# Plan's deadlines shifted by groups, scores of two batches turned by transposes, plan's durations set anew

## The chip, the cores and the metric

The kernel runs on one core of a Trainium2 chip. The metric is the device time of one execution in microseconds (us). The engines are named as in the profile: PE is TensorE (PEld its weight loads), ACT is ScalarE, DVE is VectorE, POOL is GpSimd, SP is SyncE, which issues all DMAs here. PSUM is the memory that PE writes its sums to, SBUF the one that the engines read their operands from.

## The reference

```python
B, H, S, Ns, D = (8, 8, 512, 32, 64)                     # x: B,H,S,D   state: B,H,Ns,D
...
scores = scale * np.matmul(x, state.transpose(0, 1, 3, 2))
a = softmax(scores)          # over Ns, max taken out, 1e-9 in the sum
xread = np.matmul(a, state)
scores2 = scale * np.matmul(state, x.transpose(0, 1, 3, 2))
a2 = softmax(scores2)        # over S
sread = np.matmul(a2, x)
attn = np.concatenate([xread, sread], axis=2)
...
x = attn.transpose(0, 2, 1, 3).reshape(B * 544, 512)     # tokens
a = x @ w_a                                              # 512 x 1536
b = x @ w_b
return (a * b) @ w_out                                   # 1536 x 512
```

`scores2` is `scores` with its two last axes exchanged. The softmaxes run along different axes of the same numbers.

## The kernel before, in words

**Numbers.** Everything is float32. The large matmuls run in a one-pass format (fp32r) that holds the high part of a number; each operand is split into a high and a low part (`p_h`/`p_l`, `at_h`/`at_l`, `g_h`/`g_l`, the two halves of `wq`, `wo`), and a product is made of three matmuls (high x high, high x low, low x high). Small matmuls, as the scores, run on plain float32.

**Two products joined.** `xread` is not made. For a batch, the state times the weights (`project`, tiles `ms` or `acc` in PSUM, then `sw_st`, `wo10`, `wo11` in SBUF) goes to DRAM (`scr`), comes back as a piece `p_raw` (`Batch.load`), and is split into `p_h` and `p_l` (`Batch.split`). Layer 1 multiplies the attention weights `at_h`, `at_l` with these pieces (`layer1`, PSUM tiles `ab`), makes `g = a * b` on ACT and DVE, and layer 2 (`layer2`, PSUM tiles `acc`) multiplies `g` with `w_out`. `VISITS` says in which order batches and chunks of the hidden width (0 to 5) are met; the 256 state rows of all batches (`States`) come last. Batch 0's chunk 0 and batch 2's chunk 1 don't go through DRAM (`direct0`, `direct1`).

**Attention** (`class Attention`, two groups `g` of four heads for each of eight batches; `attend`). For batches 0 and 1 (`WIDE`) the scores are made twice: `scores` gives them with the 32 states on partitions and 512 tokens along the row (PSUM tile `ms`, two matmuls 64x512), `scores_t` gives the same numbers with tokens on partitions (eight matmuls 128x64). From the second, `soft_t`, `exp`, `norm` and `back_t` make `at_h` and `at_l`, with PE turning them back by transposes against `ident`. From the first, `soft` makes `e2`, `reads` turns it by four transposes into `a2`, `sread` multiplies it with `x_nat` and `keep` puts the result into `xst`. The other six batches make the scores once, and DVE turns them in blocks of 32.

**What sets the order.** The program is recorded first, one `Unit` per instruction or per group that must stay together, with an engine, a duration `occ` and a latency `lat` from `cost`. `plan` builds the dependences, gives each unit a latest start `late` (backwards from the layer matmuls, whose due times `base` are paced), and then runs forward: on each engine it takes, among the units that can start, the one with the smallest `late`. The instructions are emitted in the order found. On the chip each engine runs its instructions in this order, so what stands ahead of a waiting instruction decides who else waits. Queues that matter here: PE, ACT, DVE, and SP for the DMAs. The pool `ps_ms` has two PSUM banks: a third group of products can start only when ACT has copied the first.

Every instruction is emitted by one line (1049), so the profile's groups are told apart by tile names. `wo` in the profile stands for `wo0` to `wo11`, and for the buffers `wo6`, `wo8` to `wo11` that other data use early.

Of the kernel before, what the change touches and what calls it, by code (L numbers as in the profile page):

```python
# [18 lines left out]
B, H, S, NS, D = 8, 8, 512, 32, 64  # L19
DM, DFF = 512, 1536  # L20
P = 128
# [143 lines left out]
class Recorder:  # L165
# [29 lines left out]
    def cost(self, u, eng, method, out, ins, kw):  # L195
        n = 1
        sh = (out if isinstance(out, View) else ins[0]).where()[0]
        for x in sh[1:]:
            n *= x
        ps = bool(ins) and ins[0].tile.pool.name.startswith("ps")  # L200
        if eng == "PE":
            if method == "transpose" or kw.get("is_transpose"):
                o = n * .85
            elif ins[-1].dtype == F32R:
                o = n * .4535
            else:
                o = n * 1.82
            if sh[0] < P:
                o *= sh[0] / P
            lat = o + 172  # L210
        elif eng == "ACT":
            if method == "activation":
                o, lat = (870, 960) if "accum_out" in kw else (560, 660)
            elif ps:
                o, lat = 466 * n / 512 + (60 if n < 300 else 0), 587 * n / 512 + (80 if n < 300 else 0)
            else:
                o, lat = 522 * n / 512, 100 + n * 1.015
            if n < 8:
                o, lat = 60, 80
        elif eng == "DVE":  # L220
            if method.startswith("tensor_scalar") and not ps:
                o, lat = (65, 140) if n <= 1 else (75, 166) if n <= 16 else (333 * n / 512, 419 * n / 512)
            elif method == "tensor_reduce":
                o, lat = 593, 676
            elif method == "transpose":
                o, lat = 628, 704
            elif method == "reciprocal":
                o, lat = (72, 154) if n == 1 else (162, 244)
            else:
                o, lat = 65 + n * 1.045, 155 + n * 1.045  # L230
        elif eng == "SP":
            o = 440
            v = out if isinstance(out, View) else ins[0]
            u.bytes = 4
            for x in v.where()[0]:
                u.bytes *= x
            u.load = isinstance(out, View) and out.tile.pool.name != "dram"
            lat = 1000 + u.bytes / 345 + (1400 if u.load else 750)
        else:
            o, lat = 1000, 1060  # L240
        if eng in ("ACT", "DVE") and out.tile.name.startswith("sd_") and len(out.where()[0]) == 4:
            o, lat = 2 * o, 2 * lat
        if eng in ("ACT", "DVE"):
            o, lat = o * SLACK, lat * SLACK
        if u.calls[:-1]:
            u.lat = u.occ + lat
            u.occ += o
        else:
            u.occ, u.lat = o, lat
# [10 lines left out]
WAKE, SLACK = 500, 1.1  # L260
# [2 lines left out]

def plan(units, pools, t0):

    n = len(units)
# [37 lines left out]
    left = [len(x) for x in suc]  # L306
    order = [i for i in range(n) if not left[i]]
    late = [0.0] * n
    end = max(u.base for u in units if u.base is not None) + 20e3
    k = 0  # L310
    while k < len(order):
        i = order[k]
        k += 1
        u = units[i]
        d = end if u.base is None else u.base + t0
        for j, wait in suc[i].items():
            d = min(d, late[j] - (0 if not wait else u.occ if units[j].eng == u.eng and u.eng != "SP" else u.lat + WAKE))
        late[i] = d
        for j in pre[i]:
            left[j] -= 1  # L320
            if not left[j]:
                order.append(j)
# [3 lines left out]
    wait = [len(x) for x in pre]  # L326
# [4 lines left out]
    done = [None] * n  # L331
    start = [None] * n
    seq, out, lanes, dma = 0, [], [], 0.0
# [5 lines left out]
    def slot(i, t):  # L339

        for x in opens.get(i, ()):
            q = slots.setdefault((x.pool, x.name), [])
            if len(q) < x.bufs:
                continue
            free_at = [max(done[j] for j in h.uses) for h in q if all(done[j] is not None for j in h.uses)]
            if not free_at:
                return None
            t = max(t, min(free_at) + WAKE)
        return t

    while len(out) < n:
        best = None
        for e in engines:
            while known[e] and known[e][0][0] <= free[e]:
                r, i = heapq.heappop(known[e])
# [5 lines left out]
            for l, i in now_ready[e]:  # L361
                t = slot(i, floor)
                if t is not None:
                    cand.append((t, l, i))
            if known[e]:
                lim = min(cand)[0] if cand else None
                for r, i in known[e]:
                    if lim is None or r < lim:
                        t = slot(i, max(r, floor))
                        if t is not None:  # L370
                            cand.append((t, late[i], i))
            if cand:
                t = min(cand)[0]
                c = min((l, i) for x, l, i in cand if x <= t + 1e-6)
# [3 lines left out]
        t, e, i = best  # L378
        u = units[i]
# [19 lines left out]
            q.append(x)  # L399
        out.append(i)  # L400
        for j, w in suc[i].items():
            r = t if not w else t + u.occ if units[j].eng == e and e != "SP" else done[i] + WAKE
            ready[j] = max(ready[j], r)
            wait[j] -= 1
            if not wait[j]:
                heapq.heappush(known[units[j].eng], (ready[j], j))
# [8 lines left out]
def attn_moe(ctx, tc, xt, xn, sd, wl, w_out, out):  # L415
# [32 lines left out]
    ident = const0.tile([P, P], F32, name="ident")  # L448
# [86 lines left out]
    w = {}  # L535
# [48 lines left out]
    def new_a(b):  # L584
        a_t[b] = [att.tile([P, NG, S], F32R, name=n, bufs=3) for n in ("at_h", "at_l")]
# [10 lines left out]
    class Attention:  # L596
# [26 lines left out]

        def scores_t(self, psp, tag):

            self.t = psp.tile([P, 512], F32, name=tag)
            self.sp = att.tile([P, 16, 32], F32, name="s_p")
            with rec.together(self.sp):
                for sb in range(4):
                    for hp in range(2):  # L630
                        c = sb * P + hp * D
                        nc.tensor.matmul(self.t[:, c:c + D], lhsT=self.x[:, hp, sb * P:(sb + 1) * P],
                                         rhs=self.st[:, hp], start=True, stop=True)

        def soft_t(self):

# [103 lines left out]
    class Batch:  # L740
        n, nk = S, NG
# [79 lines left out]
    class States:  # L821
        n, nk, begun = B * NS, 4, False
# [36 lines left out]
    units = [Batch(b) for b in range(B)] + [States()]  # L859
# [77 lines left out]
    def attend(b):  # L937
        if b not in a_t:
            new_a(b)
        for g in range(NG):  # L940
            a = atts[b, g]
            a.load()
            if b in WIDE:
                a.scores_t(*ms)
                a.scores()
                a.soft_t()
                a.exp()
                a.norm()
                a.back_t(*ms)
                a.soft()  # L950
            else:
                a.scores()
                a.soft()
                a.exp()
                a.norm()
                a.back()
            a.nat()
            a.reads()
            a.sread()
            a.keep()  # L960
# [81 lines left out]
    for p in prev:  # L1042
        layer2(*p)
        flush()
    order, start = plan(rec.units, pools, T0)
    with tc.manual_schedule():
        for i in order:
# [44 lines left out]
```

## Time and profile before

| | |
|---|---|
| median of 3 runs | 728.1 us (725.89 to 730.09) |
| the profiled execution's own time | 728.81 us |
| its span, first to last instruction | 727.0 us |
| granted TensorE clock, mean | 0.990 |
| matmul records, DVE, ACT instructions | 3440, 947, 723 |
| DMA | 134.32 MB, 185 GB/s over the span |

A row of the timeline has the start, the time from start to end of the instructions merged in it, the engine, the operation with its tiles (out<-in) and shapes, and how many. In brackets stands the idle time of the engine just before and what ended it. A matmul of 512 columns overlaps its neighbours, so its length is more than its distance to the next. A float32 matmul has two records. A clock of 0.91 in a window of 20 us means that PE ran at half clock for a part of it.

### The profile page before, as it was taken

To read this page: it belongs to the slowest core of one execution; us is meant where nothing else is said; L and a number is where in the kernel's file an instruction comes from. 1 tells how busy PE (TensorE), PEld (TensorE's weight loads), DVE (VectorE), ACT (ScalarE), POOL (GpSimd) and SP (SyncE) were. 2 spreads that over 40 slices of the span, in tenths; PEclk is the share of its full clock that TensorE was granted. 3 is DMA by queue.
4 is the path that set the end of the run, shared out by engine and by line. 5 is a ranking of instruction groups with operands and counts; after the bars stand their busy time and mean duration, and the time that the engine had idled before them with its cause. 6 is when DMAs were issued, how large, how long until landed. Compare 5 with 4: busy or idle time off the path is not lost.

```text
span 727.0 us, 9629 instructions
## 1 busy us (share of the span) xinstructions
PE 699.6 (96%) x3440; PEld 559.9 (77%) x3440; DVE 495.3 (68%) x947; ACT 395.1 (54%) x723; POOL 0.7 (0%) x6
## 2 busy tenths in 40 slices
PE   5798899999899999999999999999999999999997
PEld 4475657787786888888888887887788888988886
DVE  4985886996756967684799547637879833795322
ACT  4965786686955459786445325334456433553222
POOL 0000000000000000000000000000000000000000
PEclk9999999999999999999999999999999999999999
DMA  8557767768979436859988134314416320611002
GB/s 335 206 210 267 249 249 251 262 238 288 318 254 325 161 118 259 282 220 313 380 325 295 53 115 124 116 59 134 165 54 205 120 59 30 200 32 30 1 0 87
DMA packets 55087, 134.32 MB, mean 185 GB/s; under 512 B 5632, under 2 KB 5632, under 8 KB 55040
## 3 DMA queue, kind: packets, MB, share of 16 engines
q1 hardware_dynamic: 55040, 133.71, 52.9%
q8 instruction: 27, 0.44, 0.2%
q14 instruction: 20, 0.16, 0.1%
HBM read 87.03 MB, written 46.66 MB: 184 GB/s over the span
## 4 chain that ended last, share of the span: by engine, by line
PE 91%; ACT 4%; DVE 3%; DMA 1%; issue 1%; SPq 0%; DVEq 0%; ACTq 0%
PE ab L1049 40%; PE acc L1049 38%; PE ms L1049 12%; ACT wq L1049 2%; DMA stg<-xt 1%; DVE t L1049 1%; DVE m L1049 1%; DVE s_p L1049 0%; ACT t L1049 0%; DVE p_l L1049 0%; ACT sd_h L1049 0%; SPq L1049 0%; ACT stg L1049 0%; ACT sw_st L1049 0%; ACT at_h L1049 0%
## 5 line engine op out<-in xcount | busy, mean ns | idle before, releaser
L1049 PE MATMUL acc<-wo,g_h 128*128 128x512 f32 x816 | 255.9, 393 | 0.2 <-DVE wo L1049 0.2
L1049 PEld LDWEIGHTS acc<-wo,g_h 128*128 128x128 f32 x816 | 151.5, 188 | 33.7 <-issue 2.3
L1049 DVE TENSOR_TENSOR a_sb<-ab,a_sb 128x512 f32<-128x512 f32 (+1 forms) x108 | 71.3, 660 | 132.0 <-PE ab L1049 124.0
L1049 PE MATMUL acc<-wo,g_l 128*128 128x512 f32 x408 | 157.4, 392 | 0.0
L1049 PE MATMUL ab<-at_h,p_h 128*128 128x512 f32 x384 | 151.6, 398 | 1.1 <-ACT p_h L1049 1.1
L1049 PE MATMUL ab<-at_l,p_h 128*128 128x512 f32 x384 | 151.3, 394 | 0.0
L1049 PE MATMUL ab<-at_h,p_l 128*128 128x512 f32 x384 | 150.2, 394 | 0.0
L1049 ACT COPY a_sb<-ab 128x512 f32<-128x512 f32 (+1 forms) x108 | 60.9, 564 | 146.2 <-PE ab L1049 145.2
L1049 ACT CAST g_h<-a_sb 128x512 fp32r<-128x512 f32 (+1 forms) x108 | 64.5, 597 | 52.1 <-DVE a_sb L1049 51.7
L1049 PEld LDWEIGHTS acc<-wo,g_l 128*128 128x128 f32 x408 | 76.5, 188 | 16.4 <-issue 1.0
L1049 PEld LDWEIGHTS ab<-at_h,p_h 128*128 128x128 f32 x384 | 72.8, 190 | 19.8 <-ACT p_h L1049 2.7
L1049 PEld LDWEIGHTS ab<-at_h,p_l 128*128 128x128 f32 x384 | 72.5, 189 | 19.6 <-issue 3.0
L1049 PEld LDWEIGHTS ab<-at_l,p_h 128*128 128x128 f32 x384 | 73.0, 190 | 16.1 <-issue 1.8
L1049 DVE TENSOR_TENSOR g_l<-a_sb,g_h 128x512 fp32r<-128x512 f32 (+1 forms) x108 | 70.8, 656 | 20.9 <-ACT g_h L1049 20.8
L1049 DVE TENSOR_TENSOR p_l<-p_raw,p_h 128x512 fp32r<-128x512 f32 x92 | 60.0, 684 | 12.5 <-ACT p_h L1049 12.5
L1049 ACT CAST p_h<-p_raw 128x512 fp32r<-128x512 f32 x92 | 52.9, 621 | 14.9 <-PE ab L1049 9.2
L1049 DVE TENSOR_SCALAR t<-t 128x512 int32<-128x512 int32 x120 | 49.9, 422 | 9.8 <-ACT t L1049 8.9
L1049 PE MATMUL ms<-wq,sd_h 128*128 128x512 f32 (+2 forms) x112 | 39.6, 425 | 7.1 <-ACT wo L1049 3.8
L1049 ACT CAST wq<-t 64x512 fp32r<-64x512 f32 (+1 forms) x64 | 39.4, 619 | 8.3 <-PE ms L1049 2.8
L1049 DVE SCALAR_TENSOR_TENSOR t<-raw,t 128x512 int32<-128x512 int32 (+1 forms) x60 | 39.7, 686 | 0.3
L1049 PE MATMUL ms<-wq,sd_l 128*128 128x512 f32 (+2 forms) x112 | 38.5, 412 | 0.0
L1049 ACT COPY wo<-ms 128x512 f32<-128x512 f32 x44 | 25.8, 591 | 11.5 <-PE ms L1049 10.9
(93 smaller groups left out, 706.9 us busy)
## 6 DMA issues: line engine op xcount, KB each, us to landing
p_raw<-scr SPq DMA_DIRECT2D x46, 512.0 KB, 4.3
scr<-sw_st SPq DMA_DIRECT2D x48, 256.0 KB, 4.1
scr<-wo SPq DMA_DIRECT2D x48, 256.0 KB, 4.2
raw<-wl SPq DMA_DIRECT2D x22, 512.0 KB, 5.7
part<-stg SPq DMA_DIRECT2D x20, 512.0 KB, 2.9
stg<-part SPq DMA_DIRECT2D x20, 512.0 KB, 6.0
out<-stg SPq DMA_DIRECT2D x34, 256.0 KB, 2.3
x_raw<-xt SPq DMA_DIRECT2D x14, 576.0 KB, 3.7
```

The costliest lines, as they stand in the source:

```text
L1049: getattr(obj, method)(*map(real, args), **{k: real(x) for k, x in kw.items()})
```

## The change

It has three parts. First, `plan`'s model: the durations of two kinds of matmul, and the latency between two dependent instructions of ACT or DVE, which is now counted in full. Second, `late` gets an offset per group of units that stand together in the recording; the offsets come out of a fixed list of 54 seeds. Third, in batches 0 and 1 the scores are made once, copied to SBUF by ACT, and turned by four transposes.

```diff
             elif ins[-1].dtype == F32R:
-                o = n * .4535
+                o = (n + 32) / 2.4
             else:
-                o = n * 1.82
+                o = 90 + n * 1.8
...
+MOVES = (
+    3000001, 3000002, 3000012, 3000024, 3000027, 3000035, 3000036, 3000048, 3000052, 3000054, 3000060, 3000078,
...
+def shifts(units):
+    group, last, n = [], None, -1
+    for u in units:
+        n += u.eng == "SP" or u.eng != last
+        last = u.eng
+        group.append(n)
+    c = [0.0] * (n + 1)
+    for seed in MOVES:
...
+        end = (.12 if draw() < .4 else .3 if draw() < .5 else 1.0) * len(c)
+        begin = int(draw() * .8 * end * .6)
+        share = 10 ** (-.5 - 2.5 * draw())
+        far = 1000 * 10 ** (1.2 * draw())
+        for k in range(len(c)):
+            if k >= end:
+                break
+            u, v = draw(), draw()
+            if k >= begin and u < share:
+                c[k] += (2 * v - 1) * far
+    return [c[k] for k in group]
...
+    shift = shifts(units)
...
-            d = min(d, late[j] - (0 if not wait else u.occ if units[j].eng == u.eng and u.eng != "SP" else u.lat + WAKE))
-        late[i] = d
+            d = min(d, late[j] - (0 if not wait else u.lat + WAKE if units[j].eng != u.eng or u.eng == "SP" else
+                                  u.occ if u.eng == "PE" else u.lat))
+        late[i] = d + shift[i]
...
-            r = t if not w else t + u.occ if units[j].eng == e and e != "SP" else done[i] + WAKE
+            r = t if not w else done[i] + WAKE if units[j].eng != e or e == "SP" else t + u.occ if e == "PE" else done[i]
...
         def scores_t(self, psp, tag):
+            sc = self.e2
+            nc.scalar.copy(out=sc, in_=self.s)
+            self.s = sc
             self.t = psp.tile([P, 512], F32, name=tag)
...
                 for sb in range(4):
-                    for hp in range(2):
-                        c = sb * P + hp * D
-                        nc.tensor.matmul(self.t[:, c:c + D], lhsT=self.x[:, hp, sb * P:(sb + 1) * P],
-                                         rhs=self.st[:, hp], start=True, stop=True)
+                    nc.tensor.transpose(self.t[:, sb * P:(sb + 1) * P], sc[:, sb * P:(sb + 1) * P], ident)
...
             if b in WIDE:
+                a.scores()
                 a.scores_t(*ms)
-                a.scores()
```

PE's first rows, before. `x_raw` and `stg` are the inputs of batch 0, `acc<-wq,p_raw` is `direct0`, `s_p` the softmax with tokens on partitions, `ab` layer 1:

```order
L1049 MATMUL ms_114<-x_raw_96 128x64 x8
L1049 MATMUL ms_123<-x_raw_96 64x512 x2
L1049 MATMUL ms_148<-stg_104,stg_100 128x64 x8
L1049 MATMUL acc_182<-wq_158,p_raw_110 32x256 x4
L1049 MATMUL ms_201<-ident_87,s_p_132 128x128 x4
L1049 MATMUL acc_212<-wq_176,p_raw_112 32x256 x4
L1049 MATMUL acc_182<-p_h_208,wo7_94 128x256
L1049 MATMUL ms_201<-at_h_223,wo7_94 128x512
L1049 MATMUL ab_233<-at_h_223,p_h_208 128x512
```

PE's first rows, after the change (`e2` holds the copied scores):

```order
L1092 MATMUL ms_114<-x_raw_96 64x512 x2
L1092 MATMUL ms_127<-ident_87,e2_121 128x128 x4
L1092 MATMUL ms_149<-ident_87,e2_121 128x128 x4
L1092 MATMUL ms_159<-stg_98,stg_100 64x512 x2
L1092 MATMUL ms_170<-x_nat_106,a2_157 64x128 x8
L1092 MATMUL ms_188<-ident_87,e2_180 128x128 x4
L1092 MATMUL acc_211<-wq_164,p_raw_108 32x256 x4
L1092 MATMUL ms_223<-ident_87,s_p_142 128x128 x4
L1092 MATMUL ms_223<-at_h_235,wo7_94 128x512
L1092 MATMUL ab_247<-at_h_235,p_h_239 128x512
```

The eight 128x64 matmuls of each group are gone, four transposes of the copied scores stand in their place, and the reads of the first group (transposes of the finished `e2`, then the product with `x_nat`) have moved ahead of the first `direct0`.

The place where the first products go to DRAM and come back. First ACT's rows before (the copies of the products to `sw_st`, `wo10` and `wo11`; `acc_441` is the last product):

```order
L1049 COPY sw_st_414<-acc_398 128x512
L1049 CAST g_h_436<-a_sb_378 128x512
L1049 COPY wo11_446<-acc_417 128x512
L1049 ACTIVATE t1_454<-wo8_261 128x512
L1049 COPY wo11_446<-acc_441 128x512
```

ACT's rows after (`acc_484` is the last product):

```order
L1092 COPY wo10_454<-acc_438 128x512
L1092 COPY a2_479<-ms_449 128x512
L1092 COPY sw_st_482<-acc_456 128x512
L1092 COPY wo11_491<-acc_474 128x512
L1092 COPY a_sb_498<-ab_337 128x512
L1092 COPY sw_st_482<-acc_465 128x512
L1092 COPY wo11_491<-acc_484 128x512
```

Then SP's queue before (`scr0_0` holds the products, `p_raw` a piece, `raw` a tile of weights to be converted, `x_nat` the tokens for an attention read):

```order
L1049 DMA x_nat_503<-xn 128x1024
L1049 DMA p_raw_516<-scr0_0_349 128x2x512
L1049 DMA p_raw_520<-scr0_0_349 128x2x512
L1049 DMA raw_527<-wl 128x2x512
L1049 DMA part0_0_564<-stg_547 128x1024
```

SP's queue after:

```order
L1092 DMA x_nat_533<-xn 128x1024
L1092 DMA raw_549<-wl 128x2x512
L1092 DMA p_raw_568<-scr0_0_444 128x2x512
L1092 DMA p_raw_572<-scr0_0_444 128x2x512
L1092 DMA part0_1_613<-stg_599 128x1024
```

On ACT a copy for the attention (`a2`) and one for layer 1 (`a_sb`) have come between the copies of the products. On SP the load of weights has moved from behind the two pieces to ahead of them.

PE's rows at the second half of chunk 2's products, before (each pair of `ms` rows is one group of products that ACT must copy away; `ab_1843` is layer 1 on a piece from DRAM):

```order
L1049 MATMUL ms_1797<-wq_1471,sd_h0_180 128x512
L1049 MATMUL ms_1797<-wq_1471,sd_l0_264 128x512
L1049 MATMUL ms_1805<-wq_1471,sd_h0_180 128x512
L1049 MATMUL ms_1805<-wq_1471,sd_l0_264 128x512
L1049 MATMUL ms_1827<-wq_1538,sd_h1_217 128x512
L1049 MATMUL ms_1827<-wq_1538,sd_l1_279 128x512
L1049 MATMUL ms_1834<-wq_1538,sd_h1_217 128x512
L1049 MATMUL ms_1834<-wq_1538,sd_l1_279 128x512
L1049 MATMUL ab_1843<-at_h_1353,p_h_1832 128x512
```

The same products after:

```order
L1092 MATMUL ms_1774<-wq_1416,sd_h0_167 128x512
L1092 MATMUL ms_1774<-wq_1416,sd_l0_231 128x512
L1092 MATMUL acc_1622<-wo2_1066,g_h_1727 128x512 x2
L1092 MATMUL acc_1652<-wo2_1066,g_h_1727 128x512 x2
L1092 MATMUL acc_1672<-wo2_1066,g_h_1727 128x512 x2
L1092 MATMUL ms_1795<-wq_1416,sd_h0_167 128x512
L1092 MATMUL ms_1795<-wq_1416,sd_l0_231 128x512
L1092 MATMUL acc_1609<-wo2_1066,g_l_1784 128x512
L1092 MATMUL ms_1802<-wq_1549,sd_h1_209 128x512
L1092 MATMUL ms_1802<-wq_1549,sd_l1_273 128x512
```

Six groups stood in a row; now layer-2 matmuls stand between them.

More of the change, by code (lines that the diff above doesn't have):

```diff
@@ L261, with draw @@
 LOOSE = ("stg",)
+MOVES = (
[5 rows of a table added]
+)
+def shifts(units):
[6 more added lines that the diff above has]
+    for seed in MOVES:
+        x = seed * 2654435761 + 12345 & 0xFFFFFFFF
+        def draw():
+            nonlocal x
+            x = x * 1664525 + 1013904223 & 0xFFFFFFFF
+            return (x >> 8) / 2.0 ** 24
+        for _ in range(4):
+            draw()
+        end = (.12 if draw() < .4 else .3 if draw() < .5 else 1.0) * len(c)
[9 more added lines that the diff above has]
+    return [c[k] for k in group]
 def plan(units, pools, t0):
```

4 rows, old and new, of the table MOVES are left out of this document.

## The prediction

> **What bounds the kernel now.** I read the page's first part, then the busy time by stretch, then TensorE's rows with what ended each wait, then the rows of the other engines at the long waits.
>
> ```profile
> PE 699.6 (96%) x3440; PEld 559.9 (77%) x3440; DVE 495.3 (68%) x947; ACT 395.1 (54%) x723; POOL 0.7 (0%) x6
> L1049 PE MATMUL acc<-wo,g_h 128*128 128x512 f32 x816 | 255.9, 393 | 0.2 <-DVE wo L1049 0.2
> 0.00:25.00 25.00, 14.17 (x61) 9.72 (x61) 15.64 (x33) 14.65 (x23) 0.70 (x6) 1.00 0.80 304
> 25.00:55.75 30.75, 27.57 (x171) 20.46 (x172) 26.62 (x53) 23.11 (x47) 0.00 (x0) 0.94 0.61 212
> 55.75:101.75 46.00, 39.69 (x213) 26.81 (x214) 32.91 (x74) 32.31 (x62) 0.00 (x0) 0.93 0.77 264
> 101.75:187.00 85.25, 82.12 (x381) 63.19 (x382) 68.49 (x133) 59.59 (x109) 0.00 (x0) 0.98 0.75 257
> 187.00:717.00 530.00, 530.00 (x2586) 434.87 (x2585) 349.52 (x654) 264.67 (x485) 0.00 (x0) 1.00 0.47 162
> 717.00:727.00 10.00, 6.06 (x32) 4.87 (x30) 2.14 (x4) 0.78 (x2) 0.00 (x0) 0.97 0.14 52
> ```
>
> The stretches (columns: stretch, length, busy time of PE, PEld, DVE, ACT, POOL, then granted clock and DMA) say where time can be had. From 187 to 717 us PE is busy for 530.00 of 530.00 us at clock 1.00: a new order of the same matmuls can gain nothing there, it can only lose. All idle time of PE lies elsewhere: 10.83 us up to 25, 3.18 to 55.75, 6.31 to 101.75, 3.13 to 187 and 3.94 at the end. Beside it stands lost clock, 0.91 to 0.98 after waits. So the span is the sum of PE's work and of what PE waits for in the first 187 us.
>
> **Part 1: scores made once, then turned.** For batches 0 and 1 the second set of score matmuls goes (eight per attention, 128x64), and four transposes of the copied scores take its place.
>
> ```profile
> 34.38 0.60 PE L1049 MATMUL ms<-ident,e 128*128 128x128 f32 x4
> 34.73 0.36 PE L1049 MATMUL acc<-p_h,wo 128*128 128x256 f32 x1
> 34.93 1.89 PE L1049 MATMUL ms<-x_raw 128*128 128x64 f32 x16
> 36.63 0.48 PE L1049 MATMUL ab<-at_h,p_h 128*128 128x512 f32 x1
> ```
>
> Start to start, eight such matmuls (16 records) hold PE for 36.63 - 34.93 = 1.70 us, and four transposes for 34.73 - 34.38 = 0.35 us. That is 1.35 us of PE per attention, 5.4 us for four; 2.7 of it (batch 1) lies where PE is nearly always busy. Batch 0's share lies in the head, where PE waits anyway. Added are four copies on ScalarE (0.59 us each, 0.48 where they follow each other: two in 1.07 us, a row below). They stand in the chain scores, copy, transposes, softmax, so in the head they lengthen it.
>
> TensorE: Matmul & The Clock Gate in the Trainium skill, section "Part 4: PE-mode transpose", speaks against this part: a 128x128 transpose takes some 275 ns in a kernel, and transposes do not count as work that releases the clock. By its time, an estimate, four cost 1.1 us and batch 1 saves 1.2 instead of 2.7 us. The rows above differ: four take 0.35 us between their neighbours. Its second half returns as a rival.
>
> **Part 2: the order at the head.**
>
> ```profile
> 4.38 5.58 PE L1049 MATMUL ms<-x_raw 128*128 128x64 f32 x20 [4.38 <-DMA x_raw<-xt]
> 10.24 3.65 PE L1049 MATMUL ms<-stg 128*128 128x64 f32 x16 [0.28 <-DMA stg<-xt]
> 19.77 1.09 PE L1049 MATMUL ms<-ident,s_p 128*128 128x128 f32 x4 [4.65 <-DVE s_p L1049]
> 22.61 0.63 PE L1049 MATMUL ab<-at_h,p_h 128*128 128x512 f32 x1
> 25.14 0.66 PE L1049 MATMUL ms<-ident,s_p 128*128 128x128 f32 x4 [1.50 <-ACT at_l L1049]
> ```
>
> PE starts when the first load lands (4.38) and reaches the first layer-1 matmul at 22.61. Followed by hand in the new order with the rows' durations, ScalarE has copy, exp, two state casts of 1.1 us each and more in front of the first `at_h`, so the first layer-1 matmul comes at about 23.0: nothing won there. But PE's waits are filled: both attention reads of batch 0 and the scores of batch 1 now stand ahead of the state products. I put the end of those products at 43.5 us; now the copy behind the last of them starts at 45.53 (next fence).
>
> **Part 3: the first piece from DRAM.** PE can start batch 0's second chunk of work only when the products have gone to DRAM and come back as `p_raw`.
>
> ```profile
> 45.53 0.59 ACT L1049 COPY wo<-acc 128x512 f32<-128x512 f32 x1 [1.10 <-PE acc L1049]
> 49.41 1.58 SPq L1049 DMA_DIRECT2D p_raw<-scr  x2
> 51.24 0.37 SPq L1049 DMA_DIRECT2D raw<-wl  x1
> 55.08 1.14 ACT L1049 CAST p_h<-p_raw 128x512 fp32r<-128x512 f32 x2 [1.00 <-DMA p_raw<-scr]
> 53.76 1.08 PE L1049 MATMUL ms<-x_raw 128*64 128x512 f32 x4
> 55.75 0.50 PE L1049 MATMUL ab<-at_h,p_h 128*128 128x512 f32 x1 [0.91 <-ACT p_h L1049]
> ```
>
> From the last product's copy (45.53) to the first matmul on its piece (55.75) pass 10.2 us. In the new order this chain gets longer twice: the last product's copy stands behind five other copies on ScalarE (5 x 0.48 = 2.4 us), and on SP the load stands behind `raw<-wl` instead of ahead of it. That load waits for VectorE to finish the tile it overwrites, and its 512 KB go first: nothing if VectorE is early, some 2 us at the 212 to 304 GB/s of these stretches; I take 1. The first matmul then comes at 43.5 + 0.2 + 10.2 + 2.4 + 1 = 57.3 us, 1.5 later than now, and PE stands still there for about 4 us, since the work that it has in between is about 9.5. But by then PE has done 3.8 us of work that now comes later: two attention reads (1.0 each, 58.96 below), scores (1.0, row 53.76) and eight transposes (0.7). **Gain to this point: 3.8 - 1.5 = 2.2 us**; ends -0.5 (the load 2.7 us later still) and 4.7 (`raw` costs nothing and the copies come in time).
>
> **Part 4: the waits behind it.**
>
> ```profile
> 58.96 1.09 PE L1049 MATMUL ms<-wo,a 128*64 128x128 f32 x16 [1.41 <-ACT e L1049]
> 60.37 0.78 PE L1049 MATMUL ms<-ident,s_p 128*128 128x128 f32 x4 [0.31 <-DVE xst L1049]
> 61.82 0.79 PE L1049 MATMUL ms<-at_h,wo 128*128 128x512 f32 x1 [0.46 <-ACT at_h L1049]
> 62.41 1.05 PE L1049 MATMUL ab<-at_h,p_h 128*128 128x512 f32 x2
> 67.97 0.39 PE L1049 MATMUL ms<-wq,sd_h 128*128 128x256 f32 x1 [0.18 <-ACT e L1049]
> ```
>
> The four waits make 2.36 us. The attention work that PE waits for here stands ahead of the piece's first use in the new order, so I take 2.0 of it as gone. From 60.4 on the rows are stretched too (two matmuls in 1.05 us at 62.41), some 1.7 us lost; but a wait of 4 us before it would cost the same again, so I count no gain of clock. **2.0 us**, ends 0 and 3.8.
>
> ```profile
> 87.17 0.39 PE L1049 MATMUL ms<-wq,sd_h 128*128 128x256 f32 x1 [2.05 <-ACT sw_st L1049]
> 88.85 0.58 PE L1049 MATMUL ms<-wq,sd_h 128*128 128x256 f32 x1 [0.24 <-ACT e L1049]
> 96.90 1.09 PE L1049 MATMUL ms<-wq,sd_h 128*32 128x512 f32 x8 [1.49 <-ACT wo L1049]
> 101.75 0.50 PE L1049 MATMUL ab<-at_h,p_h 128*128 128x512 f32 x1 [0.18 <-ACT p_h L1049]
> ```
>
> Here PE waits 3.96 us for ScalarE to empty one of the two `ms` banks: six groups of products stand within 3.2 us of PE's work. After the first wait matmuls run at half clock until 91.2 (1.2 us lost). In the new order a group starts 1.2 to 3.3 us of PE's work behind the one before it (its rows counted at 0.22 us for 512 columns: two matmuls take 0.61 us in the row at 722.44 below, one 0.39). I take 4.2 of these 5.2 us; ends 1 and 5.2, since ScalarE stays loaded (32.31 of 46.00 us).
>
> ```profile
> 179.33 0.50 PE L1049 MATMUL ms<-wq,sd_h 128*128 128x512 f32 x1 [0.27 <-ACT sw_st L1049]
> 180.57 0.50 PE L1049 MATMUL ms<-wq,sd_h 128*128 128x512 f32 x1 [0.50 <-ACT sw_st L1049]
> 183.66 0.80 PE L1049 MATMUL ms<-wq,sd_h 128*128 128x512 f32 x1 [2.36 <-ACT wo L1049]
> 184.25 0.63 PE L1049 MATMUL ms<-wq,sd_l 128*128 128x512 f32 x1
> 183.02 1.07 ACT L1049 COPY wo<-ms 128x512 f32<-128x512 f32 x2
> ```
>
> This is the clearest place. Six product groups stand back to back, and ScalarE puts five steps of a weight conversion between their copies, so the fifth group waits until 183.02. The waits make 3.13 us. Behind them single matmuls take 0.63 us where 0.39 is the mean, for 3.4 us: 1.6 us more. The new order, counted likewise, has 0.2 to 2.5 us of matmuls between such groups, and the piece from DRAM that follows them is wanted 18 us of PE's work after its last product, not 5. I take 4.2 of 4.7; ends 1 and 4.7.
>
> TensorE: Matmul & The Clock Gate in the Trainium skill, section "Why this matters for your kernels", asks for no idle gap above some 3 us to keep the clock. The rows at 60.37 and 184.25 differ: waits of 1.41 and 2.36 us were enough to lose it. By the rule those stretches would have kept their clock, and part 4 would have 2.4 us less to win.
>
> **Part 5: the end.**
>
> ```profile
> 722.44 0.61 PE L1049 MATMUL acc<-wo,g_l 128*128 128x512 f32 x2
> 722.87 1.29 DVE L1049 TENSOR_TENSOR stg<-acc,stg 128x512 f32<-128x512 f32 x2 [2.47 <-PE acc L1049]
> ```
>
> Both last sums end together, so VectorE adds them one behind the other (1.29 us). In the new order the first is finished five matmuls earlier: 0.4 us less. The longer second layer that now closes the program gives ScalarE and VectorE 2.9 us of matmuls to make the last `g` in, and they need about 2: no new wait.
>
> **The plan's other edits** (durations, the latency between two instructions of one engine, the shifts) put no instruction in; they act through the order alone. Against all this stands what I couldn't follow row by row: new waits, above all in the 530 us that have none. Between 0 and 6 us; I take 1, as the distance between product groups and from products to pieces there is like before's.
>
> **Sum:** 2.2 + 2.0 + 4.2 + 4.2 + 0.4 - 1.0 = 12.0 us; the 2.7 us of batch 1 are within the first term. The span goes from 727.0 to 715.0. The profiled execution took 728.81, 1.8 over its span, and is 0.7 above the median of 728.1: 715.0 + 1.8 - 0.7 = **716 us**.
>
> **Rivals.**
> - *All waits go, and the load from DRAM is in time:* each term at its good end, 4.7 + 3.8 + 5.2 + 4.7 + 0.4 = 18.8 us, 709. For it: no two product groups on ScalarE's tight places are pressed together any more. Against: the load behind `raw`. 0.18.
> - *The waits only move:* ScalarE is as loaded as before and has four copies more, so PE waits for it at other places. Left are the 2.7 us of batch 1 and little else: 724 to 726. For it: 32.31 of 46.00 us busy on ScalarE in the worst stretch. 0.12.
> - *The head stays at half clock:* transposes take the place of matmuls up to 20 us. The rows up to 22.61 already run at half clock (0.63 for one matmul). If transposes don't keep the clock up, one or two more spells of 3.4 us cost 1.7 each: 718 to 719. The skill's transpose section, above, says so of the clock. 0.08.
> - *Slower:* the first load from DRAM. Each us by which that piece is late is paid in full, since PE's order is fixed and its next row needs it. With 12 us of other gains, and 3.6 more to be seen, it decides from 15.6 us: the piece would have to come at 73 instead of 57, through `raw<-wl` waiting that much longer for VectorE. Then 732. VectorE is busy 26.62 of 30.75 us there, which makes some delay likely and such a one not. 0.04.
>
> The forecast itself has 0.58. **The range** is 707 to 724: the good ends give 709, and head gains that I bounded too tightly a little less; all bad ends together (-0.5 + 0 + 1 + 1 - 6) give 732, and up to 724 leaves about 2 in 10 out on both sides. A measurement of this kernel can tell about 0.5%, 3.6 us, from no change; faster means under 724.5: 0.90 (forecast, first and third rival, half of the second), within 0.06, slower 0.04.
>
> **What would show it.** Right: no wait of PE for ScalarE's copies above 1 us between 70 and 190 us; the stretch from 190 to 715 still full; one wait of 3 to 5 us for `p_h` near 57 us; about 64 records of 128x64 gone. Wrong: a wait of over 2 us in a place that has none now, PE idle after 190 us, or the first layer-1 matmul later than 25 us.

## The result and the profile after

The changed kernel takes 706.1 us, median of four runs (705.07 to 709.38), the kernel before beside it on the same chip 727.2 (725.89 to 730.09): a ratio of 0.9711, interval 0.969 to 0.9732. That is 21 us faster where 12 were forecast, and 0.9 us below the range. The profiled execution took 705.07 us with a span of 703.3; its difference from before's profiled one (span 727.0) is 23.7 us, some 2.6 more than between the medians.

The first part of the page, then the busy time by stretch (columns as before: stretch, length, busy time of PE, PEld, DVE, ACT, POOL, granted clock, DMA):

```profile
PE 686.8 (98%) x3392; PEld 549.6 (78%) x3392; DVE 487.2 (69%) x947; ACT 395.1 (56%) x727; POOL 0.7 (0%) x6
0.00:25.00 25.00, 14.07 (x62) 7.00 (x63) 16.88 (x38) 17.95 (x31) 0.70 (x6) 0.85 0.86 325
25.00:55.75 30.75, 28.73 (x181) 20.18 (x179) 27.73 (x64) 26.93 (x56) 0.00 (x0) 0.96 0.84 290
55.75:101.75 46.00, 46.00 (x265) 33.20 (x264) 42.48 (x91) 38.56 (x72) 0.00 (x0) 1.00 0.84 291
101.75:187.00 85.25, 85.25 (x389) 69.26 (x387) 68.08 (x128) 66.55 (x121) 0.00 (x0) 1.00 0.82 289
187.00:693.00 506.00, 506.00 (x2467) 414.53 (x2467) 329.38 (x622) 243.03 (x446) 0.00 (x0) 1.00 0.46 155
```

From 55.75 us on PE does not wait until the tail, and its clock is full. PE's idle time over the span is 16.5 us instead of 27.4: 10.9 us of the 23.7. Its busy time fell by 12.8. Of this 5.4 are matmul work that is gone (16 records of 128x64 at 0.106 us less four transposes at 0.0875, four times). The other 7.4 us are work that runs in less time. Some 4.4 of them are clock: before had three stretches at half clock behind 55 us, with 2.94, 3.16 and 3.39 us of busy time in them, and 0.46 of that is lost (the last section has the 0.46); the changed kernel has none there.

What is left stands at the head. Some of PE's rows there, with what ended each wait:

```profile
10.24 1.11 PE L1092 MATMUL ms<-ident,e 128*128 128x128 f32 x4 [2.17 <-ACT e L1092]
20.77 0.80 PE L1092 MATMUL ms<-at_h,wo 128*128 128x512 f32 x1 [1.41 <-ACT at_h L1092]
21.67 1.22 PE L1092 MATMUL ab<-at_h,p_h 128*128 128x512 f32 x2
41.86 0.28 PE L1092 MATMUL acc<-wq,sd_l 128*128 128x256 f32 x1
53.86 0.49 PE L1092 MATMUL ab<-at_h,p_h 128*128 128x512 f32 x1 [0.17 <-ACT p_h L1092]
```

The first layer-1 matmul starts at 21.67 (22.61 before), the last product of states and weights at 41.86, and the first matmul on the piece from DRAM at 53.86 (55.75 before), after a wait of 0.17 us. The chain between the last two, from the rows of ACT and SP (`acc` is a product, `a_sb` a copy for layer 1):

```profile
42.18 0.59 ACT L1092 COPY a_sb<-ab 128x512 f32<-128x512 f32 x1
42.66 0.61 ACT L1092 COPY sw_st<-acc 128x512 f32<-128x512 f32 x1
43.13 0.62 ACT L1092 COPY wo<-acc 128x512 f32<-128x512 f32 x1
43.90 0.55 SPq L1092 DMA_DIRECT2D scr<-wo  x1
46.16 0.38 SPq L1092 DMA_DIRECT2D raw<-wl  x1
47.88 1.75 SPq L1092 DMA_DIRECT2D p_raw<-scr  x2
53.19 1.14 ACT L1092 CAST p_h<-p_raw 128x512 fp32r<-128x512 f32 x2 [0.65 <-DMA p_raw<-scr]
```

The last copy starts 1.0 us after PE has ended the last product (41.86 + 0.28). From that copy to the first matmul on the piece pass 10.7 us, 0.5 more than before.

### The profile page after: what moved, and what is told of

Same layout as the page of the kernel before. It is cut to its first block, busy times and chain, and to the rows that moved or that the text cites. A ratio compares the mean times of both kernels' runs of the same rounds, so it can differ in the third digit from the quotient of the medians.

```text
span 703.3 us, 9548 instructions
## 1 busy us (share of the span) xinstructions
PE 686.8 (98%) x3392; PEld 549.6 (78%) x3392; DVE 487.2 (69%) x947; ACT 395.1 (56%) x727; POOL 0.7 (0%) x6
## 4 chain that ended last, share of the span: by engine, by line
PE 94%; ACT 2%; DMA 2%; DVE 1%; issue 0%; SPq 0%
PE ab L1092 42%; PE acc L1092 40%; PE ms L1092 12%; DMA raw<-wl 1%; DMA p_raw<-scr 1%; ACT wq L1092 1%; DMA scr<-wo 1%; ACT sd_h L1092 1%; ACT t L1092 0%; DVE t L1092 0%; ACT e L1092 0%; SPq L1092 0%; ACT p_h L1092 0%; ACT a L1092 0%; DVE sd_l L1092 0%
## 5 line engine op out<-in xcount | busy, mean ns | idle before, releaser
L1092 PE MATMUL ab<-at_h,p_h 128*128 128x512 f32 x384 | 148.8, 395 | 0.3 <-ACT p_h L1092 0.2
L1092 PE MATMUL acc<-wo,g_l 128*128 128x512 f32 x408 | 149.0, 393 | 0.0
L1092 PE MATMUL ab<-at_l,p_h 128*128 128x512 f32 x384 | 148.9, 393 | 0.0
L1092 PE MATMUL ab<-at_h,p_l 128*128 128x512 f32 x384 | 147.6, 392 | 0.0
L1092 PE MATMUL ms<-wq,sd_h 128*128 128x512 f32 (+2 forms) x112 | 37.7, 409 | 0.0
L1092 DVE TENSOR_TENSOR stg<-acc,stg 128x512 f32<-128x512 f32 x44 | 29.2, 686 | 6.5 <-PE acc L1092 6.3
```

The source lines that it names most:

```text
L1092: getattr(obj, method)(*map(real, args), **{k: real(x) for k, x in kw.items()})
```

## The experiments

Twelve kernels ran. Runs 1 to 5 and 11 take the change apart, runs 6 to 8 keep its order and disturb one place, runs 9, 10 and 12 price waits and a single place of before's order.

**1. No shifts.**

```diff
-MOVES = (3000001, 3000002, ...
+MOVES = ()
```

> The changed kernel with an empty list of shifts: scores made once and the plan's new durations stay, the order comes out of the plan undisturbed. Theory A (the shifts pull product groups apart, and that removes PE's waits for ScalarE and the lost clock behind them): the scores' 5.4 us of PE work stay won, but in this order four product groups stand within 1.4 us of PE's work about 134 us into it, so a wait of 2 to 4 us with lost clock behind it comes back there and others in the head: 716 to 724 us. Rival B (scores and durations make the gain, the shifts are trimming): 706 to 710 us, with no PE wait above 1 us between 55 and 190 us.

729.4 us, ratio to before 1.0009 (0.9989 to 1.0028): nothing is left of the gain. Rival B falls, and theory A's range was still too good. The work of PE is that of the changed kernel, the waits are not (PE's rows):

```profile
60.10 1.09 PE L1086 MATMUL ms<-ident,s_p 128*128 128x128 f32 x4 [5.58 <-DVE s_p L1086]
179.73 0.50 PE L1086 MATMUL ab<-at_h,p_h 128*128 128x512 f32 x1 [1.89 <-ACT p_h L1086]
306.55 0.50 PE L1086 MATMUL ab<-at_h,p_h 128*128 128x512 f32 x1 [2.54 <-ACT p_h L1086]
```

PE idles 33.1 us (span 729.2, busy 696.1), twice the 16.5 of the changed kernel. Against the kernel before PE idles 5.7 us more and is busy 3.5 us less: what the missing matmuls save has turned into waits, some of them behind 190 us, where before had none.

**2. The scores part alone**, put into the kernel before.

```diff
-                a.scores_t(*ms)
                 a.scores()
+                a.scores_t(*ms)     # now: copy by ACT, four transposes
```

> The kernel before with the scores part alone (durations, latency rule and no shifts as before). Theory A: PE has 5.4 us less work, of which the part of batch 1 and some of batch 0 show; waits between 55 and 190 us stay: 720 to 726 us, PE busy time about 5 to 6 us under before's 699.6. Rival B (the transposes themselves free the head): 712 to 718 us.

727.7 us, ratio 0.9995 (0.9969 to 1.002). PE's busy time is 694.2, as expected 5.4 below before's, and its idle time 31.4, 4.0 above: work taken from PE is given back as waits when the order isn't found for it. Both theories were too hopeful.

**3. The plan's durations and latencies alone.**

```diff
-                o = n * .4535
+                o = (n + 32) / 2.4
...
```

> The kernel before with the plan's new durations and latency rule alone: no shifts, scores made twice. Theory A: the same PE work as before, another order with clusters of its own (four product groups within 1.4 us of PE's work at 139 us into it): 724 to 733 us, no clear gain. Rival B (better durations let the plan see ScalarE's tight places): 712 to 718 us.

735.0 us, ratio 1.0097 (1.0066 to 1.0129): slower, 2 us beyond the range of theory A. Rival B, which expected a gain, falls. Durations nearer to the trace don't make a better order by themselves.

**4. The changed kernel with the old scores.**

```diff
-                    nc.tensor.transpose(self.t[:, sb * P:(sb + 1) * P], sc[:, sb * P:(sb + 1) * P], ident)
+                    for hp in range(2):
+                        ...nc.tensor.matmul(self.t[:, c:c + D], lhsT=self.x[:, hp, ...], rhs=self.st[:, hp], ...)
```

> The changed kernel with the scores part undone: scores made twice, new durations, and the same seeds, which now fall on other groups of instructions. Theory A in its narrow form (the seeds were fitted to one list of instructions): 718 to 735 us, PE waits of over 1 us in places that the changed kernel fills. Wide form (any spreading of product groups helps): 709 to 713 us, that is the changed kernel plus the 5.4 us of matmuls at most.

736.0 us, ratio 1.0112 (1.0088 to 1.0136), with a single wait of 5.99 us for `p_h` at 376 us. The narrow form holds (1 us beyond its range): the same instructions without seeds took 735.0 (run 3), so the seeds fit one list of instructions and are worth nothing on this other one.

**5. Shifts in the first part only.**

```diff
-    return [c[k] for k in group]
+    cut = .3 * len(c)
+    return [c[k] if k < cut else 0.0 for k in group]
```

> The changed kernel with the shifts set to zero behind the first 30% of the groups, so that the plan's due times are disturbed in the first part of the program alone. Theory A (all of the gain is made in the first 190 us, where PE waits; behind it there is nothing to win): 704 to 712 us, and PE waits no more between 55 and 187 us than in the changed kernel. Rival B (the shifts behind 190 us carry part of the gain, since without any shift PE also waited 3.7 us between 187 and 690): 712 to 722 us with new waits behind 190 us.

712.8 us, ratio 0.9786 (0.9753 to 0.982): in rival B's range and 0.8 us above theory A's. Against the run without shifts (729.4) the early shifts give 16.6 us and the later ones the other 6.7. Theory A falls: without the later shifts PE waits behind 160 us again, and behind 187 us it idles 1.9 us (busy 511.08 of 513.00 up to 700), as rival B had it.

```profile
163.36 0.50 PE L1093 MATMUL ms<-wq,sd_h 128*128 128x512 f32 x1 [0.68 <-ACT sw_st L1093]
288.77 0.50 PE L1093 MATMUL ab<-at_h,p_h 128*128 128x512 f32 x1 [0.56 <-ACT p_h L1093]
```

**6. The first piece from DRAM late.** In the changed kernel's order SP issues `p_raw` behind the two stores that follow it.

```diff
+    at = keep.index(sp[first + 3]) + 1      # SP: behind both part<-stg
+    order = keep[:at] + [sp[first], sp[first + 1]] + keep[at:]
```

> The changed kernel with its order as it is, but SP loads the first piece from DRAM behind two stores that wait for ScalarE: its issue moves from 47.9 to about 52.4 us, its landing from 53.2 to about 57. Theory (each us by which that piece is late is paid in full, and clock behind it): PE waits 3.5 to 4 us for p_h near 57 us, and the time is 3.5 to 5.5 us longer, 709.6 to 711.6. Rival (the delay is caught up, since PE's later waits shrink): within 1 us of the changed kernel.

712.6 us, 6.5 more than the changed kernel, beyond the theory's 5.5. PE's rows at the place:

```profile
58.53 0.80 PE L1105 MATMUL ab<-at_h,p_h 128*128 128x512 f32 x1 [5.21 <-ACT p_h L1105]
62.45 0.80 PE L1105 MATMUL ms<-at_h,wo 128*128 128x512 f32 x1
64.25 1.09 PE L1105 MATMUL ms<-wo,a 128*64 128x128 f32 x16
```

The piece is used 4.7 us later (58.53 for 53.86), and all of it is paid. The wait also costs the clock: from this matmul to the attention read at 64.25 pass 5.7 us, in the changed kernel 3.5 (53.86 to 57.34). 4.7 + 2.2 = 6.9, of which 6.5 reach the end.

**7. The weight load behind the piece.** SP issues `raw<-wl` behind both `p_raw`.

```diff
+    order.remove(sp[first - 1])
+    order.insert(order.index(sp[first + 1]) + 1, sp[first - 1])
```

> The changed kernel with its order as it is, but SP issues the weight load that stands ahead of the first piece from DRAM behind it. The prediction put 1 us on that load. Theory (it costs the piece under 1 us, and PE waits only 0.17 us there, because ScalarE and VectorE end their part at the same time): the piece lands 0.3 to 1 us earlier, first matmul on it at most 0.2 us earlier, time within 0.5 us of the changed kernel. Rival (the load is what the whole chain waits for): 1 to 2 us faster.

705.9 us, ratio 0.969 (0.9657 to 0.9723), no difference from the changed kernel. The piece doesn't even land earlier: SP and ACT rows,

```profile
48.02 0.90 SPq L1103 DMA_DIRECT2D p_raw<-scr  x2
48.97 0.46 SPq L1103 DMA_DIRECT2D raw<-wl  x1
53.18 1.14 ACT L1103 CAST p_h<-p_raw 128x512 fp32r<-128x512 f32 x2 [1.09 <-DMA p_raw<-scr]
```

`p_raw` is issued at 48.02 as soon as the products are in DRAM, and its cast starts at 53.18, as it did with the 512 KB ahead of it (53.19); the first matmul on the piece starts at 53.85 (53.86). The load cost nothing.

**8. Matmuls in the place of the transposes.** The order of the changed kernel, with eight 128x64 matmuls on the copied scores instead of four transposes.

```diff
+            for h in range(2):
+                u.calls.append((obj, "matmul", (out[:, h * D:(h + 1) * D],),
+                                dict(lhsT=src, rhs=src[:, :D], start=True, stop=True)))
```

> The changed kernel with its order as it is, but in place of each four transposes of the scores of batches 0 and 1 stand eight 128x64 matmuls of the old shape on the same data, so that the attention of these two batches isn't computed. Theory (part 1 of the prediction: 1.35 us of PE per attention; in this order PE has little idle time to hide it): 2.7 to 5.4 us longer, 708.8 to 711.5. Rival (the scores part is worth nothing by itself, as in the run with that part alone, since PE waits there anyway): within 1 us of the changed kernel.

708.1 us, 2.0 above the changed kernel and 2.2 above run 7: less than the theory's 2.7, more than the rival's 1. In the profile PE is busy 693.0 us, 6.2 more, and idle 13.4, 3.1 less: batch 0's share lies in waits of the head. So the exchange of matmuls for transposes is worth 2 to 3 us in this order; the whole scores part is worth nothing in before's (run 2).

**9. Gaps in the full stretch.** GpSimd copies 64 columns of an operand onto itself between two matmuls that read it.

```diff
+            for _ in range(gaps.get(i, 0)):
+                x = real(rhs[i])[:, :64]
+                base.gpsimd.tensor_copy(out=x, in_=f32(x))
```

> The changed kernel with twelve gaps put into PE's full stretch behind 250 us: between two first-layer matmuls of one group GpSimd copies 64 columns of their common operand onto itself, 1, 1, 2, 2, 3, 3, 4, 5, 6, 8, 12 and 16 times, so that the second matmul waits for that long. The values stay as they are. Theory (a wait of PE costs its own length, and above some 1.4 us the clock too, 1.6 to 2.2 us more): rows of a 128x512 matmul behind the short gaps stay at 0.39 us, behind the gaps above 1.4 us they show 0.6 for 3 to 4 us. Rival (a wait of 1.4 to 2.4 us is not enough; before's slow rows had another cause, such as the many short waits ahead of them): rows behind gaps of up to 3 us stay at 0.39.

736.2 us. Of the twelve gaps eleven show in PE's rows (19.3 us in sum, 0.39 to 4.70). PE's rows at three of them:

```profile
545.31 0.50 PE L1108 MATMUL ab<-at_h,p_l 128*128 128x512 f32 x1 [2.98 <-POOL at_h L1106]
...
546.60 0.39 PE L1108 MATMUL ab<-at_l,p_h 128*128 128x512 f32 x1
547.21 0.63 PE L1108 MATMUL acc<-wo,g_h 128*128 128x512 f32 x1
...
549.34 0.63 PE L1108 MATMUL ab<-at_h,p_l 128*128 128x512 f32 x1
550.70 0.39 PE L1108 MATMUL acc<-wo,g_l 128*128 128x512 f32 x1
...
565.12 0.50 PE L1108 MATMUL ab<-at_h,p_l 128*128 128x512 f32 x1 [2.23 <-POOL at_h L1106]
...
623.85 0.79 PE L1108 MATMUL ab<-at_h,p_l 128*128 128x512 f32 x1 [4.70 <-POOL at_h L1106]
```

Behind 1.33, 1.43 and 2.23 us no row is slow: the theory's threshold is wrong. Behind 2.98 us the matmuls run at full clock for 1.5 us more, and only then at half clock, for 3.4 us; 3.50 us gives the same picture. Behind 4.70 us they are slow at once, for 5 us. Of the 30 us that this kernel takes longer than the changed one, 19.3 are these waits and 5.4 the clock (3.4 + 3.4 + 5.0 us, 46% of each lost); the rest isn't assigned.

**10. One place of before's order mended by hand** (ACT, 180 to 185 us; the fence gives the order of its steps by the tiles they write, not the code).

```diff
-wq, wq, t1, wq, wo10 (copy), wo10 (copy), wq, p_h, p_h
+wo10 (copy), wo10 (copy), p_h, p_h, wq, wq, t1, wq, wq
```

> The kernel before with one place of ScalarE's order changed, at 180 to 185 us: the two copies that empty the product banks and the two casts of the piece from DRAM go ahead of five steps of weight conversion. All other engines' orders stay. Theory of the prediction (ScalarE's steps make the wait of 2.36 us and the lost clock behind it): both go, 3 to 4 us faster, 723.3 to 724.3. Rival (the piece from DRAM that stands behind the products is the deadline: its last product was copied at 175.7, its load issued at 179.97, so it lands at about 184.5 whatever ScalarE does): the wait moves three matmul groups on, to the first use of p_h near 185 us, and the time is within 0.8 us of before.

733.6 us, ratio 1.0078 (1.0052 to 1.0104): slower, which neither theory had. PE's rows there, the casts on ACT, then VectorE's rows:

```profile
178.58 0.50 PE L1069 MATMUL ms<-wq,sd_h 128*128 128x512 f32 x1 [0.18 <-ACT wo L1069]
181.71 0.50 PE L1069 MATMUL ab<-at_h,p_h 128*128 128x512 f32 x1 [2.40 <-ACT p_h L1069]
187.39 0.80 PE L1069 MATMUL ab<-at_h,p_l 128*128 128x512 f32 x1 [4.47 <-DVE p_l L1069]
```

```profile
181.04 1.14 ACT L1069 CAST p_h<-p_raw 128x512 fp32r<-128x512 f32 x2 [2.51 <-DMA p_raw<-scr]
```

```profile
184.18 0.89 DVE L1069 TENSOR_SCALAR t<-t 128x512 int32<-128x512 int32 x2 [5.55 <-ACT t L1069]
186.65 2.49 DVE L1069 TENSOR_TENSOR p_l<-p_raw,p_h 128x512 fp32r<-128x512 f32 x4
```

The wait of 2.36 us for the bank is gone (0.18 stands before the next group), and 2.40 us come back two product groups later, for the piece: ACT itself waits 2.51 us for it to land, the rival's mechanism. Then comes a second wait, 4.47 us: VectorE runs its steps in its old order, and the steps of the weight conversion that wait for the ACT steps now moved back stand ahead of `p_l`. The waits at the place make 7.8 us instead of 3.1, and behind the second one single matmuls take 0.63 us up to 192.7. Here one engine's order couldn't be mended without the others'.

**11. Half of the seeds.**

```diff
-MOVES = (...)
+MOVES = (...)[:27]
```

> The changed kernel with the first 27 of the 54 seeds. Theory (each seed was kept for one wait that it removed, so gains add up over the list): between the run without shifts and the changed kernel, 710 to 722 us, with PE waits left between 25 and 190 us. Rival (most of the gain is in a few large seeds at the front): 706 to 709 us.

712.1 us, ratio 0.978 (0.976 to 0.9801), in the theory's range: 17.3 us from the first half of the list, 6.0 from the second. The gain is spread over the list, and its first half is worth more; no seed was priced alone.

**12. Gaps set close together**, made as in run 9.

> The changed kernel with gaps again (GpSimd copies an operand of first-layer matmuls onto itself between them), now set close together, with some 0.5 us of matmuls between two of one place: about 1.4 + 1.4 us, 0.8 + 0.8 + 0.8, 1.4 + 1.4 + 1.4, 2.2 + 0.8, and by themselves 2.2, 2.7, and 0.8 + 0.8. In the run with single gaps, 1.43 and 2.23 us cost no clock, while 2.98 and 3.50 each brought 3.4 us of matmuls at 0.43 us instead of 0.23, beginning 1.4 to 1.9 us behind the gap. Theory (what counts is PE's idle time summed over some 4 us, so that before's 0.27 + 0.50 + 2.36 us lost the clock although none of them would alone): the places with 3 us or more in sum (1.4 x3, 2.2 + 0.8) show slow rows, those with up to 2.4 us don't, 1.4 + 1.4 lies between. Rival (only the length of the single longest gap counts): none of the places shows slow rows except perhaps 2.7.

One execution, 743.3 us. PE's rows at two of the places:

```profile
313.79 0.74 PE L1113 MATMUL ab<-at_h,p_l 128*128 128x512 f32 x2 [1.03 <-POOL at_h L1111]
315.55 0.50 PE L1113 MATMUL ab<-at_h,p_h 128*128 128x512 f32 x1 [1.03 <-POOL at_h L1111]
316.35 0.56 PE L1113 MATMUL acc<-wo,g_l 128*128 128x512 f32 x1
316.71 0.63 PE L1113 MATMUL ms<-wq,sd_h 128*128 128x512 f32 x1
...
319.99 0.40 PE L1113 MATMUL ab<-at_l,p_h 128*128 128x512 f32 x1
...
450.06 0.50 PE L1113 MATMUL ab<-at_h,p_l 128*128 128x512 f32 x1 [2.23 <-POOL at_h L1111]
451.75 0.51 PE L1113 MATMUL ab<-at_h,p_l 128*128 128x512 f32 x1 [0.73 <-POOL at_h L1111]
452.10 0.40 PE L1113 MATMUL ab<-at_h,p_h 128*128 128x512 f32 x1
```

Two gaps of 1.03 us cost the clock for 3.4 us, while 2.23 + 0.73 and 1.22 + 0.88 + 0.72 cost none; 1.59 + 1.29, 2.94 + 0.83 + 0.83 and single gaps of 2.91 and 3.25 cost it. Neither the sum nor the longest gap decides, so theory and rival both fall. Much of it is where a gap falls; the last section shows against what.

## Why the prediction was wrong in size

The direction and the mechanism held: PE's waits between 55 and 187 us go, the full stretch behind stays full, the clock comes back. The sum was short, term by term:

| term | predicted | measured | from |
|---|---|---|---|
| up to the first piece | 2.2 | 6.1 | 4.2 of work done earlier + (55.75 - 53.86) |
| waits behind it, 59 to 68 us | 2.0 | 3.8 | 2.36 of waits and 1.4 of clock (0.46 of 2.94) gone |
| waits for banks, 87 to 102 us | 4.2 | 5.4 | 3.96 of waits and 1.5 of clock (0.46 of 3.16), none left |
| cluster at 179 to 187 us | 4.2 | 4.7 | none left |
| tail | 0.4 | 0.4 | idle 3.94 to 3.56 |
| new waits | -1.0 | 0 | PE 506.00 of 506.00 busy |

The work done earlier is counted in the two traces: two attention reads (2.0), one group's scores (1.0) and 14 transposes (1.2 with the narrow ones), where the prediction had eight. Of clock in the second row the prediction read 1.7 us off the rows; the busy time at half clock allows 1.4.

The measured terms make 20.4 us, against 21 between the medians and 23.7 between the two profiled executions. The 3.3 us left in the profile may be what a wait costs beyond its bracket: a row of 128x512 lasts 0.39 us where the next one starts after 0.23, so a bracket leaves out 0.16, and the first matmul behind a wait takes 0.33 us to the next (180.57 to 180.90 in the kernel before) instead of 0.23. For the eleven waits that are gone between 55 and 187 us that is an estimate of 2.9 us.

**The step that failed** is part 3, the time of the first matmul on the piece: "43.5 + 0.2 + 10.2 + 2.4 + 1 = 57.3 us", measured 53.86. It failed in three places. The products end 1.4 us earlier than the 43.5 followed by hand (41.86 + 0.28 = 42.1), as the first layer-1 matmul does (21.67, not 23.0). Of the 0.2 + 2.4 us for the copies 1.0 was there. In the kernel before the last copy started as its product ended: ScalarE at 45.53, and PE's row of the last product,

```profile
45.22 0.28 PE L1049 MATMUL acc<-wq,sd_l 128*128 128x256 f32 x1
```

(the 1.10 in the bracket at 45.53 is idle time of ScalarE ahead of that). Now the last copy stands behind `a_sb` and `sw_st` (42.18 and 42.66) and starts 1.0 us after the product. The rest of the "five other copies" cost nothing: a product takes PE 0.96 us (eight matmuls, 0.12 each), a copy ACT 0.48, so they run while PE makes the products. Position in a queue was read as lateness. And the load behind `raw` was given 1 us; the way from the last copy to the matmul is 0.5 us longer than before, and run 7 shows that none of it is that load's. So 1.4 us of products, 1.6 of copies and 0.5 of the load (1 less the 0.5 that came) were put in too much: 3.5 us, within rounding the difference between 57.3 and 53.86. The wait of 4 us that followed from 57.3 was 0.17, and with it went the reason for not counting the clock in the next term. The good end of the term (4.7) was too tight as well, since no part of it allowed for an earlier head.

**Part 1** was right for the transposes (0.0875 us each, PE's busy time 6.2 us longer in run 8) and for the share that shows: 2.7 predicted, 2 to 3.1 measured. But runs 1 and 2 show that it shows only in an order that uses it.

**Part 4** was right that the waits go; the allowances at two places (1.0 and 0.5 us) weren't needed. Its reason was incomplete. The prediction put the cluster at 179 us down to ScalarE and named the distance from the last product to the piece, 18 us of PE's work instead of 5, in passing. Run 10 shows that the second stands behind the first: with ScalarE's copies in time PE waits just as long for the piece.

**The clock**: the prediction read from before's rows that "waits of 1.41 and 2.36 us were enough to lose it". The lengths alone don't decide: in run 9 single waits of 1.43 and 2.23 us lose nothing. By the grid of the last section the waits of 1.41 and 0.31 us lie in one of its stretches, 57.35 to 60.76 (1.72 us idle), and the wait of 2.36 us lies whole in another, 180.23 to 183.64 (2.68 us idle with part of the 0.50 ahead of it). The loss of 1.6 us there is right as a sum. The rule that the prediction set against those rows (the Trainium skill, "TensorE: Matmul & The Clock Gate", section "Why this matters for your kernels": no idle gap above some 3 us) fits the single gaps of run 9, 2.23 us kept and 2.98 lost, but not the pair of 1.03 us in run 12.

**New waits and the rivals.** No new wait came behind the piece. The rival's price was right: run 6 makes the piece 4.7 us late and all of it is paid, with 2.2 us of clock on top. The result is nearest to the first rival, "all waits go, and the load is in time" (709); its own bound on part 3 was the one that failed. That the waits only move, the second rival, is what happens in runs 1, 2 and 10, so it was given too little as a mechanism, though the changed kernel avoids it: its order fits this one list of instructions (runs 4, 5 and 11). The third rival's half clock is there: the granted clock is 0.50 from 17.48 to 27.72 us. But the kernel before had it up to 23.2 us and again from 30.04 to 33.45, so nothing was lost against it.

No version was found that beats the changed kernel; run 7 equals it. What remains, 10.9 us of idle time before 25 us, wasn't tried.

## What to carry to other kernels

Where PE is the bound and its order is fixed, taking work off it or mending one wait can be worth nothing by itself, as in runs 2 and 10: the time comes back as a wait at the next thing with a deadline, here a trip through DRAM or a step on another in-order engine. Follow a place to its real deadline before pricing it, and count a queue ahead of an instruction as delay only if that queue is slower than what feeds it. An order fitted to one list of instructions has to be fitted again when the list changes.

## What the runs showed of the hardware

The granted clock changes on a fixed grid. A row of a single 128x512 matmul that lies between 0.229 us (full) and 0.427 us (half clock) from the next can be split into its two parts, which dates the change. In run 12, beside the row at 316.35 above:

```profile
524.62 0.61 PE L1113 MATMUL ab<-at_h,p_h 128*128 128x512 f32 x1
525.03 0.63 PE L1113 MATMUL ab<-at_l,p_h 128*128 128x512 f32 x1
572.08 0.56 PE L1113 MATMUL acc<-wo,g_h 128*128 128x512 f32 x1
572.47 0.40 PE L1113 MATMUL ab<-at_l,p_h 128*128 128x512 f32 x1
```

The changes lie at 316.43, 524.64 and 572.43 us: the second and third 208.21 and 256.00 us behind the first, which is 61.0 and 75.0 times 3.413 us. In the kernel before, these rows date two changes back to full clock to 91.51 and 187.07, 28.0 times 3.413 apart:

```profile
91.16 0.55 PE L1049 MATMUL ab<-at_h,p_l 128*128 128x512 f32 x1
91.55 0.39 PE L1049 MATMUL ab<-at_l,p_h 128*128 128x512 f32 x1
...
186.81 0.51 PE L1049 MATMUL ab<-at_l,p_h 128*128 128x512 f32 x1
187.16 0.39 PE L1049 MATMUL ab<-at_h,p_l 128*128 128x512 f32 x1
```

The profile's granted clock agrees: it is 0.50 from 316.43 to 319.83 in run 12, and up to 91.47 and 187.05 in the kernel before.

Laid over this grid, most gaps of runs 9 and 12 sort themselves. By the profile's busy times, stretches of 3.413 us in which PE idles 1.81 (the two gaps of 1.03 us, 313.01 to 316.42), 1.87 or 1.94 us are followed by one at half clock; those with 1.49 us (360.80 to 364.21, behind the gap of 1.22) and 1.71 us (446.13 to 449.54, most of the gap of 2.23) aren't. The limit is not sharp in this measure. At the end of run 9 a stretch with 1.83 us (727.77 to 731.18) keeps the clock, and in run 2 one with 1.40 us (80.40 to 83.81) loses it; what else counts stays open. In all traces every stretch at full clock with 1.87 us of idle time or more, 55% of it, is followed by half clock. That is why two gaps of 1.03 us can cost 1.6 us (3.41 us at half speed, 1 - 0.229/0.427 = 0.46 of it) and a gap of 2.23 us that lies across a boundary costs nothing. Transposes counted as work here: in run 5 PE is busy for 1.87 us between 51.01 and 54.42, of which two groups of four transposes make 1.26; without them PE would have idled for 2.8 us, and the clock stayed full. The Trainium skill, "TensorE: Matmul & The Clock Gate", section "Part 1: The HAM clock gate (the "warmup" mystery)", says that the clock follows a free-running window of 4096 cycles, about 3.4 us, and these runs agree; it has the clock fall after an idle window, where here a window that is idle for 55% was enough.
